# Thirteen buffers for the attention rows, stores issued later, and the turned keys copied by ScalarE

## The chip, the cores and the metric

The kernel is one program on one core of a Trainium2 chip. The metric is device time in microseconds (us), from a launch with all inputs in device memory to the last output row. Before the change the median of three runs is 881.03 us (880.51 to 882.46).

## What the kernel computes

Three stages in a row, on 3072 tokens of 384 features (4 batches x 768 positions, 8 heads of 48):

```
# 1. gated linear attention, per batch and head
f = 1 / (1 + exp(-f_logit))
state = f[t][:, None] * state + k[t] outer v[t]        # 48 x 48, t = 0..767
y[t] = q[t] @ state
# 2. mixture of 8 experts with a fixed capacity of 384 tokens
x = y as rows [3072, 384];  logits = x @ w_gate
assign tokens greedily, best logits first, until each expert has 384
out[tokens of e] = relu(x[tokens of e] @ w1[e]) @ w2[e]
# 3. a dense layer pair on all tokens
h = x @ w_in;  g = h * tanh(log(1 + exp(h)));  g @ w_out
```

Inputs are float32 but for `w_in` and `w_out`, which arrive as 8-byte floats and are split into a high and a low part on the chip.

## The kernel before

The attention stage takes the first 164 us. It walks through 24 units; unit u is a pair (chunk c of 128 positions, batch b), c = u // 4 and b = u % 4. A unit has these steps, each a few instructions: the gates (`gate1`, `gate2`: exponential, minimum, logarithm of the gate inputs, split into `sphi` and `splo`), their running sum on TensorE (`cum`), two exponentials of it (`ep`, `kp`), the products with q and k on GpSimd, the turning of both (`trans`: eight 128x128 transposes into two PSUM tiles, then copies to `qT` and `kT`), the scores `sc` = kT x qT, their mask `scm`, the output `y`, the state's update, and `rows`, which turns the output back into token rows, writes the logits to `L` and the rows through `xs` to `x_rows` in device memory.

The steps of several units are interleaved. In the loop over u a string of letters, `ORD = "tcHOkEPyrCseimaQSnNoxDpMdb"`, is the order in which work is given to the engines in one unit: a small letter with a step beside it emits TensorE work, and the capital and other letters flush work that was deferred (a copy out of PSUM, a mask). So unit u emits the transposes of u+1, the running sum of u+2, the rows of u-1, the output of u and the scores of u+1. Every engine runs its own instructions strictly in this order.

The parts that the change touches:

- `trans` (line 413): the copy to `qT` is deferred under letter H and done by ScalarE (line 423); the copy to `kT`, under letter O, is done by VectorE (line 424). In VectorE's list it stands behind the splitting of the 8-byte weights (lines 84 to 86) and behind one step of `fill` (lines 153 to 176, constants for the routing), which end the unit before, and ahead of the reduction to `L`, the gates' minimum, the state's addition (line 468) and `sphi` (line 361).
- `rows` (line 475): `xs` has two buffers, and the store of 128 rows of 1536 bytes is issued at once, in unit u for the rows of u-1.
- The loop head (lines 546 to 551): the loads of `f` for unit u+6, of q, k and v for u+4 and a piece of the 8-byte weights, all on SyncE's queue, as are the stores and the small transfer `decs` (line 379), which brings the last row of `ep` to four partitions. At b = 2 `dec` (line 384) reads four such rows of a chunk.

Transfers issued by SyncE take eight completion semaphores in turn: each issue first waits until the transfer eight places before it has landed.

After the attention a branch on `flag` picks a slow path that these inputs don't take. The routing then sorts out the tokens of the first expert, gathers their rows from `x_rows` (line 907) and the expert stage runs to the end.

Of the kernel before, what the change touches and what calls it, by code (L numbers as in the profile page):

```python
# [7 lines left out]
F32 = mybir.dt.float32  # L8
# [5 lines left out]
AF = mybir.ActivationFunctionType  # L14
# [216 lines left out]
def tile_gated_attention(ctx, tc, q, k, v, f_logit, w_gate, x_d, L, flag, ident, fill, one, w64, choices):  # L231
# [5 lines left out]
    nc = tc.nc  # L237
    B, H, S, D = q.shape
    C = 128
    NC = S // C  # L240
    DP = 64
    NP = H // 2
# [4 lines left out]
    work = ctx.enter_context(tc.tile_pool(name="a_work", bufs=2))  # L247
# [5 lines left out]
    NU = len(units)  # L253
# [22 lines left out]
    def load_f(u):  # L276
        if u >= NU:
            return
        f = work.tile([128, H, D], F32, name="f", bufs=4)
        nc.sync.dma_start(f, src(f_logit, u))  # L280
        F[u] = f

    def load(u):
        if u >= NU:
            return
        kk = work.tile([128, H, D], F32, name="kk", bufs=3)
        qq = work.tile([128, H, D], F32, name="qq", bufs=3)
        nc.sync.dma_start(qq, src(q, u))
        nc.sync.dma_start(kk, src(k, u))
        LD[u] = (kk, qq)  # L290

    def load_v(u):
        if u < NU:
            nc.sync.dma_start(vv[u % NV], src(v, u))
# [46 lines left out]
    def misc(shape):  # L341
        return psum.tile(shape, F32, name="misc", bufs=2)
# [24 lines left out]
    def cum(u):  # L367
        c, b = units[u]
        kk, qq = LD[u]
        hi, lo = SP[u]  # L370
        pc = psum.tile([128, H, D], F32, name="cum")
        pcf = pc.rearrange("p h d -> p (h d)")
        nc.tensor.matmul(pcf, trir, hi, start=True, stop=False)
        nc.tensor.matmul(pcf, trir, lo, start=False, stop=True)
        def exps():
            ep = epad[u % 2]
            nc.scalar.activation(ep[:, :, :D], pc, AF.Exp, scale=-1.0)
            nc.scalar.activation(kpad[u % 3][:, :, :D], pc, AF.Exp)
            (nc.scalar if u < 4 else nc.sync).dma_start(decr[c % 2][b:b + 1], ep[127:128])
            defer("P", lambda: (nc.vector if u < 2 else nc.gpsimd).tensor_mul(qpad[u % 2][:, :, :D], qq, ep[:, :, :D]))  # L380
            defer("Q", lambda: (nc.vector if u < 1 else nc.gpsimd).tensor_mul(kpad[u % 3][:, :, :D], kk, kpad[u % 3][:, :, :D]))
        defer("E", exps)

    def dec(c):
        V = nc.vector
        r = slice(c % 2 * 32, c % 2 * 32 + B)
        V.tensor_scalar(fjunk[r], decr[c % 2][:, :, :D], 1e-34, None, op0=OP.is_ge, op1=OP.min,
                        accum_out=flg[r, c:c + 1])
        V.tensor_scalar(flg[r, c:c + 1], flg[r, c:c + 1], -1.0, 1.0, op0=OP.mult, op1=OP.add)
        if c == NC - 1:  # L390
            return
        p = misc([128, NP, B])
        for j in range(NP):
            nc.tensor.transpose(p[:, j, :], decr[c % 2][:, 2 * j:2 * j + 2, :].rearrange("b h d -> b (h d)"), ident[r, r])
        d = work.tile([128, NP, B], F32, name="dec")
        V.tensor_copy(d, p)
        DEC[c] = d
# [10 lines left out]
    def set_flag2(m):  # L408
        p = misc([1, 1])
        nc.tensor.matmul(p, m, ident_ones, start=True, stop=True)  # L410
        nc.vector.tensor_scalar(flag, p, 1.0, None, op0=OP.min)

    def trans(u):
        pq = psum.tile([128, NP, 128], F32, name="tr", bufs=2)
        for j in range(NP):
            nc.tensor.transpose(pq[:, j, :], qpad[u % 2][:, 2 * j:2 * j + 2, :].rearrange("p h d -> p (h d)"), ident)
        pk = psum.tile([128, NP, 128], F32, name="tr", bufs=2)
        for j in range(NP):
            nc.tensor.transpose(pk[:, j, :], kpad[u % 3][:, 2 * j:2 * j + 2, :].rearrange("p h d -> p (h d)"), ident)
        qT = work.tile([128, NP, 128], F32, name="qT")  # L420
        kT = work.tile([128, NP, 128], F32, name="kT")
        QT[u], KT[u] = qT, kT
        defer("H", lambda: nc.scalar.activation(qT, pq, AF.Copy))
        defer("O", lambda: nc.vector.tensor_copy(kT, pk))

    def scores(u):

# [12 lines left out]
    def yout(u):  # L440
        c, b = units[u]
        p = py


        for j in range(NP):
            for s in range(2):
                nc.tensor.matmul(p[s * DP:s * DP + D, j], vv[u % NV][:, 2 * j + s, :], SC[u][:, 2 * j + s, :],
                                 start=j == 0, stop=not c and j == NP - 1)
        for j in range(NP if c else 0):
            for s in range(2):  # L450
                r = slice(s * DP, s * DP + D)
                nc.tensor.matmul(p[r, j], St[b][r, j, :], QT[u][r, j, :], start=False, stop=j == NP - 1)
        def copy():
            xT = work.tile([128, NP, 128], F32, name="xT", bufs=1)
            nc.scalar.activation(xT, p, AF.Copy)
            XT[u] = xT
        defer("x", copy)

    def state(u):
        c, b = units[u]  # L460
        if c == NC - 1:
            return
        p = misc([128, NP, DP])
        for h in range(H):
            s, j = h % 2, h // 2
            nc.tensor.matmul(p[s * DP:(s + 1) * DP, j, :D], kpad[u % 3][:, h, :],
                             vv[u % NV][:, h, :], start=True, stop=True)
        defer("a", lambda: nc.vector.tensor_add(St[b], St[b], p[:, :, :D]))

    def decay(u):  # L470
        c, b = units[u]
        nc.gpsimd.tensor_mul(St[b], St[b], DEC[c][:, :, b:b + 1].to_broadcast([128, NP, D]))

    def rows(u):

        c, b = units[u]
        p = misc([128, NP, PW])
        for j in range(NP):
            nc.tensor.matmul(p[:, j, :], XT[u][:, j, :], pick[:, j, :], start=True, stop=True)
        def store():  # L480
            xs = work.tile([128, NP, 2 * D], F32, name="xs")
            nc.scalar.activation(xs, p[:, :, :2 * D], AF.Copy)
            r0 = b * S + c * C
            nc.sync.dma_start(x_d[r0:r0 + C, :], xs.rearrange("p j d -> p (j d)"))
        defer("r", store)
        defer("C", lambda: nc.vector.tensor_reduce(L[:, b * NC + c, :], p[:, :, 2 * D:].rearrange("p j e -> p e j"),
                                                   axis=AX.X, op=OP.add))
# [4 lines left out]
    def defer(letter, fn):  # L492
        if now[0] or letter not in ORD:
            fn()
        else:
            pend.setdefault(letter, []).append(fn)

    def flush(letter=None):
        for l in list(pend) if letter is None else [letter]:
            while pend.get(l):  # L500
                pend[l].pop(0)()
# [39 lines left out]
    for u in range(NU):  # L541
        c, b = units[u]
        if u == 3:
            filling = fill(jp)
        if u >= 3 and b != 2:
            next(filling, None)
        load_f(u + 6)
        load(u + 4)
        load_v(u + 4)
        if u >= 3:  # L550
            w64.step("load")
        now[0] = False
        for o in ORD:
            flush(o)
            if o in 'mbp' and u < 3:
                continue
            if o == 'm':
                w64.step("magnitude")
            if o == 't' and u + 1 < NU:
                trans(u + 1)  # L560
            if o == 'c' and u + 2 < NU:
                cum(u + 2)
            if o == 'b':
                w64.step("bits")
                if u == last:
                    w64.step("parts")
            if o == 'y':
                yout(u)
                if u == last:
                    set_flag2(far)  # L570
            if o == 's':
                state(u)
            if o == 'D' and b == 2:
                dec(c)
            if o == 'e':
                gates(min(u + 5 - (u < 2), NU), 0)
            if o == 'n':
                gates(0, min(u + 4, NU))
            if o == 'k' and u:
                rows(u - 1)  # L580
            if o == 'p':
                w64.step("parts")
            if o == 'S' and u < last:
                scores(u + 1)
            if o == 'd':
                decays(u)
        if u == NU - 2:
            far = set_flag()
    flush()
    now[0] = True  # L590
    for _ in filling:
        pass
    rows(NU - 1)
    for _ in choices.steps(work.tile([128, H, D], F32, name="qq", bufs=3).rearrange("p h d -> p (h d)")):
        pass
    while not w64.done():
# [740 lines left out]
```

## Time and profile before

| | us |
|---|---|
| median of three runs | 881.03 (880.51 to 882.46) |
| the profiled execution | 884.77 |
| its span, first to last instruction | 882.8 |
| TensorE busy | 821.2 (93%) |
| VectorE busy | 680.2 (77%) |
| ScalarE busy | 541.8 (61%) |
| GpSimd busy | 401.8 (46%) |

Times in the traces are those of the one profiled execution. "Busy" is an average over stages; in the slices of the page the DMA engines are full (digit 9) only in the first six of 40, which is the attention stage. A wait that a view names is put down to the semaphore that came last.

### The profile page before, as it was taken

How to read it: one execution, taken by the hardware profiler on the slowest of the kernel's cores; microseconds unless marked ns; L12 is line 12 of the kernel's file. 1: busy time of each engine (PE TensorE's matmuls, PEld its weight loads, DVE VectorE, ACT ScalarE, POOL GpSimd, SP SyncE). 2: the span in 40 equal slices, each digit the busy share in tenths (PEclk: the TensorE clock that was granted, in tenths of full speed). 3: DMA queues.
4: the chain of work that ended last, by engine and by line, in shares of the span. 5: the costliest groups of instructions: out<-in, count | busy, mean ns of one | idle time of the engine just before them, and what ended most of it. 6: DMA issues, size and time to landing. Idle time of an engine off the chain costs nothing.

```text
span 882.8 us, 16971 instructions
## 1 busy us (share of the span) xinstructions
PE 821.2 (93%) x6162; PEld 766.9 (87%) x6162; DVE 680.2 (77%) x1734; ACT 541.8 (61%) x1283; POOL 401.8 (46%) x395
## 2 busy tenths in 40 slices
PE   7989999548999999999999999999999999999996
PEld 6878888446888889999989998899889899999995
DVE  5668898778799869876987798779877885765564
ACT  5656666215378538754774587467637764884684
POOL 4657788134237423641464155415532643545143
PEclk9999999768999999999999999999999999999999
DMA  9999995253330003001300210030004105100000
GB/s 166 200 225 218 215 220 135 84 157 120 130 104 27 1 28 144 27 10 29 133 28 19 103 60 19 28 143 19 9 29 144 27 1 171 27 1 25 4 1 27
DMA packets 127862, 71.97 MB, mean 82 GB/s; under 512 B 102944, under 2 KB 120352, under 8 KB 127776
## 3 DMA queue, kind: packets, MB, share of 16 engines
q1 hardware_dynamic: 124576, 61.41, 26.3%
q0 software_dynamic: 3072, 9.44, 3.4%
q8 instruction: 50, 0.82, 0.4%
q14 instruction: 36, 0.29, 0.1%
q10 hardware_dynamic: 128, 0.01, 0.0%
HBM read 61.35 MB, written 9.44 MB: 80 GB/s over the span
## 4 chain that ended last, share of the span: by engine, by line
PE 51%; issue 9%; POOL 9%; DVE 5%; DMA 3%; ACT 2%; POOLq 0%; SPq 0%; DVEq 0%; ACTq 0%
PE h L947 17%; PE h L945 9%; PE acc L947 8%; POOL gl L1014 6%; PE acc L1069 4%; PE acc L945 4%; PE acc L1064 4%; PE acc L1065 4%; DMA xg<-x_rows,idx 2%; POOL xg L907 1%; POOL w1l L915 1%; DVE cmp L696 1%; PE misc L773 1%; DMA w1r<-in_moe_w_dram 1%; ACT gh L1005 1%
## 5 line engine op out<-in xcount | busy, mean ns | idle before, releaser
L1014 POOL TENSOR_TENSOR gl<-g,gh 128x384 fp32r<-128x384 f32 x127 | 162.8, 1282 | 288.9 <-ACT gh L1005 284.3
L945 PE MATMUL h<-yh,winh 128*128 128x384 f32 x384 | 132.5, 345 | 0.3 <-DVE g L995 0.2
L1064 PE MATMUL acc<-wouth,gh 128*128 128x384 f32 x384 | 130.1, 339 | 1.1 <-ACT gh L1005 0.5
L947 PE MATMUL h<-yh,winl 128*128 128x384 f32 x384 | 129.4, 337 | 0.0
L1065 PE MATMUL acc<-woutl,gh 128*128 128x384 f32 x384 | 129.4, 337 | 0.0
L947 PE MATMUL h<-yl,winh 128*128 128x384 f32 x384 | 129.3, 337 | 0.0
L1034 DVE SCALAR_TENSOR_TENSOR e<-e,r 128x384 f32<-128x384 f32 (+2 forms) x154 | 78.2, 522 | 34.7 <-ACT r L1029 34.2
L963 ACT ACTIVATE h1h<-h 128x384 fp32r<-128x384 f32 x64 | 31.4, 491 | 112.8 <-PE h L947 112.7
L915 POOL TENSOR_TENSOR w1l<-w1r,w1h 128x384 fp32r<-128x384 f32 x64 | 67.4, 1054 | 72.4 <-ACT w1h L914 72.4
L1069 PE MATMUL acc<-wouth,gl 128*128 128x384 f32 x384 | 89.5, 341 | 1.8 <-POOL gl L1014 1.7
L1022 ACT ACTIVATE e<-e 128x384 f32<-128x384 f32 (+2 forms) x154 | 69.5, 468 | 29.9 <-DVE e L1043 27.8
L1005 ACT ACTIVATE gh<-g 128x384 fp32r<-128x384 f32 (+2 forms) x154 | 69.0, 464 | 28.4 <-DVE g L995 27.8
L1047 DVE SCALAR_TENSOR_TENSOR e<-e,r 128x384 f32<-128x384 f32 (+2 forms) x154 | 82.2, 548 | 0.2
L1040 ACT ACTIVATE e<-h 128x384 f32<-128x384 f32 (+2 forms) x154 | 62.7, 424 | 23.7 <-PE h L947 23.7
L1064 PEld LDWEIGHTS acc<-wouth,gh 128*128 128x128 f32 x384 | 72.0, 188 | 4.5 <-ACT gh L1005 4.5
L995 DVE SCALAR_TENSOR_TENSOR g<-e,h 128x384 f32<-128x384 f32 (+2 forms) x154 | 71.8, 480 | 4.1
L1043 DVE TENSOR_SCALAR e<-e 128x384 f32<-128x384 f32 (+2 forms) x154 | 58.5, 391 | 21.3 <-ACT e L1040 21.1
L945 PEld LDWEIGHTS h<-yh,winh 128*128 128x128 f32 x384 | 72.5, 189 | 1.7 <-issue 0.7
L947 PEld LDWEIGHTS h<-yl,winh 128*128 128x128 f32 x384 | 72.2, 188 | 0.8
L1069 PEld LDWEIGHTS acc<-wouth,gl 128*128 128x128 f32 x384 | 67.3, 188 | 5.9 <-POOL gl L1014 5.3
L1065 PEld LDWEIGHTS acc<-woutl,gh 128*128 128x128 f32 x384 | 72.1, 188 | 0.0
L947 PEld LDWEIGHTS h<-yh,winl 128*128 128x128 f32 x384 | 72.0, 188 | 0.0
(239 smaller groups left out, 2052.2 us busy)
## 6 DMA issues: line engine op xcount, KB each, us to landing
w1r<-in_moe_w_dram SPq DMA_DIRECT2D x8, 1536.0 KB, 6.4
w2r<-in_moe_w_dram SPq DMA_DIRECT2D x8, 1536.0 KB, 9.6
f<-in_f_logit_dram SPq DMA_DIRECT2D x24, 192.0 KB, 3.8
qq<-in_q_dram SPq DMA_DIRECT2D x24, 192.0 KB, 4.2
kk<-in_k_dram SPq DMA_DIRECT2D x24, 192.0 KB, 4.5
vp<-in_v_dram SPq DMA_DIRECT2D x24, 192.0 KB, 4.4
x_rows<-xs SPq DMA_DIRECT2D x24, 192.0 KB, 3.2
cv_raw<-in_moe_w_in_dram SPq DMA_DIRECT2D x9, 384.0 KB, 4.3
```

Of the source, the lines that this page charges most:

```text
L915: nc.gpsimd.tensor_sub(al, s, ah.bitcast(F32))
L945: nc.tensor.matmul(p, wh, xh, start=start, stop=False)
L947: nc.tensor.matmul(p, w, x, start=False, stop=stop and w is (wh if late_x else wl))
L995: nc.vector.scalar_tensor_tensor(g[:, c], s2[:, c], 0.5, p[:, c], op0=OP.add, op1=OP.mult)
L1005: nc.scalar.activation(gh[:, c], g[:, c], AF.Copy)
L1014: nc.gpsimd.tensor_sub(gl, g, gh.bitcast(F32))
L1022: nc.scalar.activation(s[:, c], s[:, c], AF.Square, bias=1.0)
L1034: nc.vector.scalar_tensor_tensor(s[:, c], s[:, c], 1.0, r[:, c], op0=OP.add, op1=OP.mult)
L1047: nc.vector.scalar_tensor_tensor(s[:, c], s[:, c], 2.0, r[:, c], op0=OP.subtract, op1=OP.mult)
L1064: nc.tensor.matmul(A[k, 1][t], gh[:, s], wouth[:, f, :], start=f == 0, stop=False)
L1065: nc.tensor.matmul(A[k, 1][t], gh[:, s], woutl[:, f, :], start=False, stop=False)
L1069: nc.tensor.matmul(A[k, 1][t], gl[:, s], wouth[:, f, :], start=False, stop=f == GB - 1)
```

## The change

The rows of up to thirteen units stay in SBUF: `xs` gets 13 buffers, and `rows` no longer issues the store but puts it on a list. From the thirteenth unit (u = 12) on, the loop head takes one store off the list per unit and issues it, behind that unit's loads; from u = 19 on it takes up to four. What is left is issued after the last rows. Apart from that the copy to `kT` goes from VectorE to ScalarE, at the same letter.

```diff
         defer("H", lambda: nc.scalar.activation(qT, pq, AF.Copy))
-        defer("O", lambda: nc.vector.tensor_copy(kT, pk))
+        defer("O", lambda: nc.scalar.activation(kT, pk, AF.Copy))
...
+    NX = 13
+    stores = []
+
+    def put_rows(n):
+        for _ in range(min(n, len(stores))):
+            nc.sync.dma_start(*stores.pop(0))
+
     def rows(u):
...
-            xs = work.tile([128, NP, 2 * D], F32, name="xs")
+            xs = work.tile([128, NP, 2 * D], F32, name="xs", bufs=NX)
             nc.scalar.activation(xs, p[:, :, :2 * D], AF.Copy)
             r0 = b * S + c * C
-            nc.sync.dma_start(x_d[r0:r0 + C, :], xs.rearrange("p j d -> p (j d)"))
+            stores.append((x_d[r0:r0 + C, :], xs.rearrange("p j d -> p (j d)")))
...
         if u >= 3:
             w64.step("load")
+        if u >= NX - 1:
+            put_rows(1 if u < NU - 5 else 4)
         now[0] = False
...
     rows(NU - 1)
+    put_rows(NU)
```

On SyncE's queue, around units 2 and 3, the instructions stood like this before (L280, L288, L289 and L294 load f, q, k and v, L60 the 8-byte weights, L379 is `decs`, L484 the store of rows):

```order
L484 DMA x_rows<-xs 128x384
L280 DMA f<-in_f_logit_dram 128x8x48
L288 DMA qq<-in_q_dram 128x8x48
L289 DMA kk<-in_k_dram 128x8x48
L294 DMA vp_103<-in_v_dram 128x8x48
L60 DMA cv_raw<-in_moe_w_in_dram 128x3x256
L379 DMA decs<-ep_113 1x16x32
L484 DMA x_rows<-xs 128x384
L280 DMA f<-in_f_logit_dram 128x8x48
```

Now the first store on this queue is that of unit 12; the end of the loop, from the loads of unit 19 on, reads so (L480 is the store):

```order
L288 DMA qq<-in_q_dram 128x8x48
L289 DMA kk<-in_k_dram 128x8x48
L294 DMA vp_104<-in_v_dram 128x8x48
L60 DMA cv_raw<-in_moe_w_in_dram 128x3x256
L480 DMA x_rows<-xs 128x384 x4
L379 DMA decs<-ep_113 1x16x32
L60 DMA cv_raw<-in_moe_w_out_dram 128x768
L480 DMA x_rows<-xs 128x384 x4
L379 DMA decs<-ep_112 1x16x32
L480 DMA x_rows<-xs 128x384 x4
L379 DMA decs<-ep_113 1x16x32
L480 DMA x_rows<-xs 128x384 x4
```

Up to unit 11 a unit's round on the queue has six transfers in place of seven; the stores of 17 of the 24 units now stand behind the last load of q, k and v.

On VectorE, around the thirteenth unit, where `fill` has its longest step (L173), the copy L424 is gone from between that step and the reduction to `L` (L486, now L494):

```order
 L86 SCALAR_TENSOR_TENSOR cv_x<-cv_x,cv_s 128x384
 L173 CAST slots<-row 128x512
-L424 COPY kT<-tr 128x512
-L486 TENSOR_REDUCE L<-misc 128x8
+L494 TENSOR_REDUCE L<-misc 128x8
 L351 TENSOR_SCALAR f<-f 128x384
 L468 TENSOR_TENSOR S_114<-S_114,misc 128x192
```

Nothing else moves in that list. On ScalarE the copy now stands right behind its twin L423 and ahead of the two exponentials of the running sum:

```order
 L423 ACTIVATE qT<-tr 128x512
+L424 ACTIVATE kT<-tr 128x512
 L377 ACTIVATE ep_113<-cum 128x8x48
 L378 ACTIVATE kp_108<-cum 128x8x48
 L379 DMA decs<-ep_113 1x16x32
-L482 ACTIVATE xs<-misc 128x384
+L490 ACTIVATE xs<-misc 128x384
 L348 ACTIVATE f,esum<-f 128x384
```

So the exponentials, and behind them the copy to `xs` and the gates, start one copy later in ScalarE's list.

## Rows read from the trace of the kernel before

**Rows 1.** The page: span, and DMA busy tenths in 40 slices

```profile
span 882.8 us, 16971 instructions
DMA  9999995253330003001300210030004105100000
```

**Rows 2.** Stretches: length, busy PE, PEld, DVE, ACT, POOL, PE clock, DMA share, GB/s

```profile
74.50:92.80 18.30, 18.30 (x253) 16.30 (x254) 14.94 (x33) 13.09 (x31) 14.48 (x16) 1.00 0.96 218
92.80:112.30 19.50, 18.30 (x251) 16.26 (x250) 18.35 (x35) 12.97 (x31) 15.69 (x18) 1.00 0.97 219
112.30:132.20 19.90, 18.10 (x247) 16.03 (x247) 18.57 (x32) 13.11 (x31) 16.05 (x18) 1.00 0.97 216
180.00:200.00 20.00, 11.11 (x104) 9.57 (x102) 14.22 (x58) 3.19 (x7) 6.23 (x7) 0.68 0.57 181
```

**Rows 3.** Waits of PE, 15 to 150 us: total, times, longest

```profile
PE sc L432 <- DVE L L486: 4.1, 6, 1.2
PE misc L394 <- issue: 2.6, 1, 2.6
PE sc L432 <- ACT wouth L107: 0.5, 1, 0.5
```

**Rows 4.** Timeline of the thirteenth unit, all engines: start, duration, instruction, wait

```profile
94.34 1.23 DVE L173 CAST slots<-row 128x512 bf16<-128x512 f32 x1
94.77 0.67 PE L466 MATMUL misc<-vp,kp 128*64 128x48 f32 x16
95.49 0.68 DVE L424 COPY kT<-tr 128x512 f32<-128x512 f32 x1
96.31 1.16 PE L432 MATMUL sc<-qT,kT 48*128 48x128 f32 x16 [0.87 <-DVE L L486]
96.72 0.35 DVE L361 CAST sphi<-f 128x384 fp32r<-128x384 f32 x1
97.21 1.00 POOL L364 TENSOR_TENSOR splo<-f,sphi 128x384 fp32r<-128x384 f32 x1 [1.93 <-DVE sphi L361]
98.51 0.34 PE L374 MATMUL cum<-splo,trir 128*128 128x384 f32 x1
```

**Rows 5.** Timeline of units 5 and 6, PE and SyncE's queue

```profile
43.20 1.08 PE L447 MATMUL y<-scm,vp 128*48 128x128 f32 x16
49.16 1.08 PE L447 MATMUL y<-scm,vp 128*48 128x128 f32 x16
51.78 1.16 PE L432 MATMUL sc<-qT,kT 48*128 48x128 f32 x16
51.85 0.51 SPq L379 DMA_DIRECT2D decs<-ep  x1
55.59 0.38 PE L394 MATMUL misc<-ident,decs 4*128 4x4 f32 x4 [2.65 <-issue]
```

**Rows 6.** Two stretches that follow waits of PE, columns as in Rows 2

```profile
55.60:60.00 4.40, 4.40 (x28) 4.20 (x30) 4.20 (x15) 1.74 (x4) 2.01 (x4) 0.61 1.08 230
69.60:74.00 4.40, 4.39 (x30) 4.18 (x31) 3.41 (x8) 0.82 (x2) 2.77 (x4) 0.61 0.86 219
```

**Rows 7.** The line of the stores, 20 to 52 us: count, ns, starts

```profile
L484 SPq DMA_DIRECT2D x_rows<-xs x4: 518/526/1999, 27.4 to 47.3; - x4
```

**Rows 8.** Timeline of the fourteenth unit: ScalarE, GpSimd and the next transposes

```profile
98.10 0.60 ACT L423 ACTIVATE qT<-tr 128x512 f32<-128x512 f32 x1 [2.20 <-PE tr L416]
98.89 0.49 ACT L377 ACTIVATE ep<-cum 128x384 f32<-128x384 f32 x1 [0.19 <-PE cum L374]
101.47 1.32 POOL L381 TENSOR_TENSOR kp<-kk,kp 128x384 f32<-128x384 f32 x1
103.77 0.66 PE L416 MATMUL tr<-ident,qp 128*128 128x128 f32 x4
```

**Rows 9.** Timeline of the stage's end: the last `xs`, then the first gather

```profile
163.79 0.49 ACT L482 ACTIVATE xs<-misc 128x384 f32<-128x384 f32 x1 [0.82 <-PE misc L479]
190.06 1.18 POOL L907 DMA_INDIRECT xg<-x_rows,idx  x1 [10.67 <-DVE th L868]
```

## The prediction

> **What bounds the kernel now.** I read the page first: the span is 882.8 us, and the DMA engines are full in the first six of 40 slices only, the attention stage [rows 1]. Everything that the change touches lies in that stage, which ends with the last copy to `xs` at 163.79 + 0.49 = 164.3 us [rows 9]. Next I cut the stage into stretches of three units each. From 74.5 to 92.8 us TensorE is busy 18.30 of 18.30 us, at full clock, with the DMA engines at 0.96; in the two stretches after it TensorE idles 1.20 and 1.80 us while VectorE is busy 18.35 of 19.50 and 18.57 of 19.90 [rows 2]. So two things run close together here: TensorE's own work and the transfers. Which one ends last must be read from TensorE's waits. An undisturbed unit is the distance between two outputs, 49.16 - 43.20 = 5.96 us, without a gap [rows 5].
>
> TensorE's waits from 15 to 150 us come third. Two kinds carry nearly everything: the scores wait for VectorE or, by the label, for ScalarE, 4.1 + 0.5 = 4.6 us in seven places, and the transposes of `decs` wait once, 2.6 us [rows 3]. The label of the scores' wait names the instruction that came last by the profile, and I read it further in the timeline: in the thirteenth unit the state's matmuls end at 94.77 + 0.67 = 95.44; the copy to `kT`, an operand of the scores, stands behind the 1.23 us step of `fill`, ends at 95.49 + 0.68 = 96.17, and the scores start at 96.31 [rows 4]. They wait for `kT`. The wait for `decs` is another story: the transfer is issued at 51.85, TensorE is through with its scores at 51.78 + 1.16 = 52.94 and starts the transposes at 55.59, 3.74 us after the issue [rows 5].
>
> Behind two of these waits there is a second loss: from 55.6 to 60.0 and from 69.6 to 74.0 us TensorE is busy throughout, but at a mean granted clock of 0.61 [rows 6]; each follows a wait, the one for `decs` and the longest of the scores (1.2 us). The two levels are 1.2 and 2.4 GHz, so 0.61 is mostly the lower one. Each stretch loses 4.4 x (1 - 0.61) = 1.7 us, if its work scales with the clock.
>
> **The change part by part.**
>
> The copy to `kT`. VectorE loses 24 copies of 0.68 us, ScalarE gains 24 of the same shape as its copy to `qT`, 0.60 us [rows 4, 8]. On VectorE the copy stood ahead of the scores; now it is done right behind `qT`, at 98.70 to 99.30 in the unit shown, over 3 us ahead of those scores. All 4.6 us of waits go [rows 3], and I expect the second stretch of low clock to go with the wait ahead of it: 1.7 us [rows 6]. What is late next is the low half of the running sum, which takes `splo` from GpSimd, which takes `sphi` from VectorE. In the thirteenth unit `sphi` ends at 97.07, 0.90 after the copy ended; without it VectorE is through with the `fill` step at 95.57 and `sphi` ends about 96.47, so `splo`, 0.14 us later and 1.00 long, ends at 97.61. TensorE takes its scores at 95.44 and, 98.51 - 96.31 = 2.20 us later, asks for `splo` at 97.64 [rows 4]. That just fits. Where VectorE's list is longer relative to TensorE's it won't, and I allow 0.6 us in all for such places; the ends are 0 and 3.0 us, the idle time of TensorE in the two stretches where VectorE is fullest [rows 2].
>
> On ScalarE the copy delays `ep` from 98.89 to 99.30, 0.41 us, since 0.19 us of waiting is used up [rows 8]. Busy time per unit was 13.09 / 3 = 4.36 us [rows 2], so 4.96 of 5.96 then. Queued behind are `kp`, `xs`, the gates and `xT`, and `ep` releases GpSimd's two products. In the unit shown the second of them ends at 101.47 + 1.32 = 102.79, while the next transposes start at 103.77 [rows 8]: 0.98 us of cover against 0.41 of delay. I cost it at nothing; if the cover is gone, the price is up to 0.41 us a unit.
>
> The stores. What they cost before is their share of a full DMA. A store is 128 x 1536 bytes = 197 KB. No row isolates it, so I bound it: at the mixed rate of the full stretches, 218 GB/s at share 0.96, it is 0.87 us; at the rate that large pieces reach later, 181 GB/s at a share of 0.57, that is 318 GB/s at full, 0.62 us [rows 2]. Its rows are large pieces, so I take 0.62. Issuing one also holds SyncE's queue 0.53 us [rows 7]. With the engines full and eight transfers under way at most, whatever is taken out ahead of a transfer brings it forward. Four stores stood ahead of the `decs` that TensorE waited for [rows 7]: at 0.62 us they are 2.5 us, at 0.87 it is 3.5. The transfer would be issued at 49.35 or earlier and land, with the same 3.74 us, at 53.09, against TensorE's 52.94 [rows 5]. I count 2.2 of the 2.65 us as gone, with 0 and 2.65 as ends, and the low clock after it gone with it, 1.7 us [rows 6].
>
> The Trainium skill, "DMA: Bandwidth & Descriptors", section Specifications, puts the ceiling of the fabric at 435 GB/s. By that a store would be an estimated 0.45 us, four 1.8, and the wait would keep some 0.8 us, so that the sum below came out 0.4 lower; the fastest stretch cited here stands at 318 GB/s, and the trace decides for the larger price.
>
> From unit 12 on one store a unit comes back, into a queue which by then has caught up, and the four per unit from 19 on stand behind the last loads. Three small losses are possible: `decs` of the last chunks stands behind four issues of 0.53 us, and the routing's first instructions wait for every landed store. I allow 0.3 us. The first gather starts at 190.06, 25.8 us after the last `xs` [rows 9]; 16 late stores at 0.62 to 0.87 us are 10 to 14 us of DMA time, spread over the last five units, so the gather doesn't see them. Everything after the stage moves as a block.
>
> Sum: 4.6 + 1.7 + 2.2 + 1.7 - 0.6 - 0.3 = 9.3 us. Against the profiled execution this is 882.8 - 9.3 = 873.5 us of span and 884.77 - 9.3 = 875.5 us in all; that execution is 3.7 us above the median of the runs, so 881.03 - 9.3 = 871.7 us is what I predict.
>
> **The rivals.**
>
> (A) The wait for `decs` stays or moves. The DMA engines remain near full, and with a faster TensorE the transfers have less time; from unit 12 on the stores are back. Then 2.2 + 1.7 us are not gained, and the change brings 5.4: 875.6 us. For it: DMA shares of 0.96 and 0.97 up to 132 us [rows 2]. Against it: removing one of seven transfers cuts a unit's demand below its 5.96 us.
>
> (B) VectorE stays the bound where GpSimd is busiest. VectorE's busy time per unit rises from 14.94 / 3 = 4.98 us to 18.35 / 3 = 6.1 and 18.57 / 3 = 6.2 as GpSimd's goes from 4.83 to 5.23 and 5.35 [rows 2]; the one long `fill` step is only 1.23 of it [rows 4]. Closer packing could stretch it again until the freed 0.68 us is eaten: the 3.0 us of idle time there stays, and the change brings 9.3 - 2.4 = 6.9: 874.1 us. Against it: 6.2 - 0.68 = 5.5 is under 5.96. The Trainium skill, "SBUF — State Buffer", section Terms, has VectorE and GpSimd arbitrate for one shared pair of ports, the loser blocked for a full instruction. By that rule the packing does stretch VectorE, and the time is the 874.1 us of this case; the rise in the rows agrees with it, as far as they go.
>
> (C) The stores pile up at the end. Sixteen are issued in the last five units and the branch's far side waits for all. If four are still queued behind the last one, 4 x 0.62 to 0.87 adds 2.5 to 3.5 us to the routing's start: 9.3 - 3 = 6.3, 874.7 us.
>
> (D) Slower. ScalarE paces the units: what `ep` loses to the copy holds GpSimd's products, these the next transposes, these the next copies, and the delay is handed on from unit to unit. It decides from the point where `ep` is late by more than the 0.98 us of cover [rows 8]; the copy alone gives 0.41, so the gates and `xT` behind it would have to slip too. Then the units, now (18.3 + 19.5 + 19.9) / 9 = 6.41 us on average [rows 2], last 0.60 us more instead of getting shorter: 20 units with a state part lose 12.0 us, the relief at `decs` still brings 3.9, and the time is 881.03 + 8.1 = 889.1 us. Against it: a ScalarE that even with the copy idles 1.0 us of each 5.96.
>
> **How the numbers follow.** The forecast with both mechanisms, a gain of 8 to 11 us, gets 0.60; A 0.15, B 0.10, C 0.06, D 0.04; 0.05 is left for something that I don't see and that leaves no change. The range runs from a gain of 11.7 us (all bounds at their best, 4.6 + 1.7 + 2.65 + 1.7 = 10.65, and 1.1 for unseen relief of the early transfers) to one of 4.2, somewhat under A: 869.3 to 876.8 us. About 0.2% of the time, 1.8 us, is what can be told from no change; faster by more gets 0.91, within it 0.05, slower 0.04.
>
> **What would show it.** Right: outputs 5.96 us apart from unit 4 to unit 20, but for some 0.3 us at each `dec`; no wait of the scores for VectorE; the wait for `decs` under 0.6 us; a granted clock of 1.00 from 20 us to the stage's end; the last `xs` at about 155 us; every later stage of its old length. Wrong: a new wait of the running sum for `splo` over 1 us in total (B), of the transposes for GpSimd (D), of `decs` in unit 10, 14 or 18 (A), or a routing that starts over 3.5 us after the last `xs` (C).

## The result

The changed kernel took 872.66 us (median of 4 runs, 871.43 to 874.92) against 880.85 us of the kernel before (4 runs): a ratio of 0.9893, 95% interval 0.9869 to 0.9917, a gain of 8.2 us. Measured again beside the later experiments it took 874.20 us against 881.46, a ratio of 0.9926 (0.9896 to 0.9955). The forecast was 871.7.

The page after: 13.1 us less span, and the DMA engines are still full in the first six slices [rows 1].

```profile
span 869.7 us, 16917 instructions
DMA  9999996362510021003100400031004105000000
```

The end of the attention stage, the last `xs` and the first gather [rows 9]:

```profile
154.85 0.49 ACT L490 ACTIVATE xs<-misc 128x384 f32<-128x384 f32 x1 [0.81 <-PE misc L487]
181.17 1.19 POOL L918 DMA_INDIRECT xg<-x_rows,idx  x1 [10.68 <-DVE th L879]
```

The stage ends at 155.34 instead of 164.28 us, 8.94 earlier, and the gather starts 8.89 earlier: the stores that are still out when the stage ends cost the routing nothing. Nothing shows that the rest of the 13.1 us belongs to the change. From the first expert's first gather to the second's, in code that did not change, the profile of before took 76.74 us and this one 72.90; over the thirteen profiles of this study that stretch took 72.2 to 76.7, in no order that follows the edits. The medians, 8.2 us apart, agree with the stage alone.

TensorE's waits from 15 to 150 us, after (total, times, longest) [rows 3], and the stretches of rows 2 between the same outputs:

```profile
PE cum L374 <- POOL splo L364: 1.2, 3, 0.6
```

```profile
74.75:93.17 18.42, 18.42 (x251) 16.26 (x250) 16.22 (x33) 14.01 (x34) 15.06 (x17) 1.00 0.95 204
93.17:111.74 18.57, 18.48 (x251) 16.27 (x250) 17.26 (x32) 14.13 (x34) 15.72 (x18) 1.00 0.93 197
111.74:129.96 18.22, 18.22 (x251) 16.26 (x250) 15.80 (x33) 13.72 (x34) 16.37 (x18) 1.00 1.00 227
...
20.00:155.00 135.00, 132.91 (x1773) 117.37 (x1770) 106.03 (x224) 97.76 (x230) 100.85 (x113) 1.00 0.91 204
```

The waits of the scores and of `decs` are gone, TensorE is busy 55.12 of the 55.21 us of the three stretches (columns: length, busy PE, PEld, DVE, ACT, POOL, PE clock, DMA share, GB/s), and its granted clock is at 1.00 from 20 us to the end of the stage. The thirteenth unit [rows 4], the copy now on ScalarE:

```profile
88.61 1.22 DVE L173 CAST slots<-row 128x512 bf16<-128x512 f32 x1
89.03 0.67 PE L466 MATMUL misc<-vp,kp 128*64 128x48 f32 x16
89.63 1.16 PE L432 MATMUL sc<-qT,kT 48*128 48x128 f32 x16
...
90.38 0.34 DVE L361 CAST sphi<-f 128x384 fp32r<-128x384 f32 x1
90.87 1.01 POOL L364 TENSOR_TENSOR splo<-f,sphi 128x384 fp32r<-128x384 f32 x1 [1.32 <-DVE sphi L361]
91.91 0.59 ACT L424 ACTIVATE kT<-tr 128x512 f32<-128x512 f32 x1
91.93 0.19 PEld L374 LDWEIGHTS cum<-splo,trir 128*128 128x128 f32 x1 [0.20 <-POOL splo L364]
```

The scores start with no gap behind the state's matmuls, while `fill`'s long step is still running on VectorE. `splo` is now what comes last, and by little: TensorE's weight load waits 0.20 us for it. In two other units it waits longer:

```profile
67.55 0.19 PEld L374 LDWEIGHTS cum<-splo,trir 128*128 128x128 f32 x1 [0.56 <-POOL splo L364]
110.50 0.19 PEld L374 LDWEIGHTS cum<-splo,trir 128*128 128x128 f32 x1 [0.35 <-POOL splo L364]
```

These waits hardly show in TensorE's busy time, in which matmuls overlap, but the three units last 6.53, 6.16 and 6.32 us from output to output in place of 5.96, 1.1 us more in all. Waits for `splo` aren't new, either. The view from which rows 3 are taken has this line too:

```profile
PE cum L374 <- POOL splo L364: 1.6, 3, 0.6
```

Those three waits of before, and two of the three after, lie in the stage's first units, up to 27 us. Units 5 and 6 [rows 5], and the stretch behind the transposes of `decs` [rows 6]:

```profile
48.65 0.50 SPq L379 DMA_DIRECT2D decs<-ep  x1
50.01 1.08 PE L447 MATMUL y<-scm,vp 128*48 128x128 f32 x16
52.63 1.16 PE L432 MATMUL sc<-qT,kT 48*128 48x128 f32 x16
53.73 0.41 PE L394 MATMUL misc<-ident,decs 4*128 4x4 f32 x4
```

```profile
53.70:58.10 4.40, 4.40 (x54) 4.07 (x54) 4.24 (x12) 3.35 (x9) 4.40 (x6) 1.00 1.06 241
```

`decs` is sent 1.36 us ahead of the unit's output, where before it was sent 2.69 behind it, and L394 doesn't wait. The same 4.4 us now hold 54 matmuls where they held 28.

### The profile page after: what moved, and what is told of

The parts are those of the page before. It is cut to its first block, busy times and chain, and to the rows that moved or that the text cites. A ratio compares the mean times of both kernels' runs of the same rounds, so it can differ in the third digit from the quotient of the medians.

```text
span 869.7 us, 16917 instructions
## 1 busy us (share of the span) xinstructions
PE 817.1 (94%) x6162; PEld 763.7 (88%) x6162; DVE 670.5 (77%) x1710; ACT 551.1 (63%) x1307; POOL 403.7 (46%) x395
## 4 chain that ended last, share of the span: by engine, by line
PE 54%; POOL 8%; issue 8%; DVE 5%; DMA 3%; ACT 2%; POOLq 0%; SPq 0%; DVEq 0%; ACTq 0%
PE h L958 18%; PE h L956 10%; PE acc L958 7%; POOL gl L1025 5%; PE acc L1080 5%; PE acc L1075 4%; PE acc L1076 4%; PE acc L956 4%; DMA xg<-x_rows,idx 2%; POOL xg L918 2%; DVE cmp L707 1%; POOL w1l L926 1%; PE misc L784 1%; DMA w2r<-in_moe_w_dram 1%; ACT e L1051 1%
```

## What the experiments showed

`decs` collects the last row of `ep` from four units; the row of the last of the four (u = 7, 11, 15, 19, with u counted from 0) is the one that L394 can be late for. The table puts all kernels side by side, each from its own profile: from the first `y` to the last `xs`, how long after the end of `ep` (L377) that unit's row was sent (L379), and how long TensorE stood for it. The ratio is to the kernel before on the same chip.

| kernel | ratio (95%) | first y to last xs | row sent after ep, u = 7, 11, 15, 19 | waits at L394 |
|---|---|---|---|---|
| before | 1 | 148.95 | 7.91, 2.71, 3.19, 2.78 | 2.65 |
| changed | 0.9893 (0.9869 to 0.9917) | 139.14 | 4.67, 2.69, 4.54, 5.57 | none |
| changed, again | 0.9926 (0.9896 to 0.9955) | 139.90 | 6.31, 4.16, 5.09, 5.97 | 0.20 |
| keys alone | 0.9959 (0.9940 to 0.9977) | 143.80 | 6.35, 5.56, 6.58, 4.38 | 0.76, 2.47 |
| stores alone | 0.9979 (0.9964 to 0.9993) | 148.81 | 7.20, 1.66, 3.52, 4.69 | 1.52 |
| VectorE's copy placed earlier | 0.9969 (0.9953 to 0.9985) | 143.24 | 7.25, 5.93, 4.97, 5.60 | 1.23, 0.58 |
| changed, 7 buffers | 0.9954 (0.9932 to 0.9976) | 145.93 | 6.55, 6.47, 5.86, 8.03 | 0.32, 2.18, 1.57 |
| keys, row by ScalarE | 0.9911 (0.9882 to 0.9941) | 140.40 | 0.03 each | none |
| row by ScalarE alone | 0.9953 (0.9930 to 0.9975) | 143.51 | 0.03 each | none |
| changed, row by ScalarE | 0.9909 (0.9877 to 0.9942) | 140.14 | 0.03 each | none |
| changed, copied twice | 0.9921 (0.9901 to 0.9941) | 142.08 | 4.17, 2.81, 3.99, 6.94 | 1.49 |
| the same, row by ScalarE | 0.9928 (0.9902 to 0.9953) | 141.20 | 0.03 each | none |
| changed, first three keys by VectorE | 0.9909 (0.9884 to 0.9934) | 140.16 | 6.04, 3.75, 4.65, 6.33 | 0.30 |

Waits under 0.1 us are left out. Every such row that was sent 6.35 us or more after its `ep` made TensorE wait, and none that was sent within 5.9 us did. In the cases with a wait TensorE was ready for the row 9.0 to 10.2 us after that `ep`, and the row took 3.5 to 5.8 us from issue to landing: it is late when standing in line and landing together take longer than TensorE leaves them.

Lengths and rows are those of one execution for each kernel; the two of the changed kernel differ by 0.76 us in length and by 1.64 us in when the row of u = 7 was sent. The ratios rest on 4 to 12 runs of each kernel.

### Keys alone

```diff
-        defer("O", lambda: nc.vector.tensor_copy(kT, pk))
+        defer("O", lambda: nc.scalar.activation(kT, pk, AF.Copy))
```

> Only the copy to kT goes to ScalarE; the stores stay as before. Theory (two separate causes): the scores' seven waits of 4.6 us go, and the low clock behind the longest with them (1.7 us); the wait for decs in unit 6 stays at 2 to 3.5 us, since it comes ahead of most of the others. Last xs ends at 157.5 to 159.5 us instead of 164.3 (155.3 with both parts), the time is some 875.5 us. Rival (the transfers set the pace): TensorE gets ahead and waits for decs in units 10, 14 or 18 too, over 1 us each; last xs after 160.5 us, time above 877.

The stage ended at 159.92 us, between the two theories, and the time, 878.62 us, was in the rival's range. TensorE's waits, its clock behind the longer of the two, and SyncE's line ahead of it:

```profile
PE misc L394 <- issue: 3.2, 2, 2.5
...
```

```profile
93.27 0.49 ACT L377 ACTIVATE ep<-cum 128x384 f32<-128x384 f32 x1
93.80 0.60 SPq L379 DMA_DIRECT2D decs<-ep  x1
...
99.64 0.60 SPq L60 DMA_DIRECT2D cv_raw<-in_moe_w_in_dram  x1
100.34 0.51 SPq L379 DMA_DIRECT2D decs<-ep  x1
106.25 0.44 PE L394 MATMUL misc<-ident,decs 4*128 4x4 f32 x4 [2.47 <-issue]
```

```profile
106.30:110.70 4.40, 4.40 (x28) 4.28 (x30) 3.16 (x9) 2.29 (x5) 2.01 (x3) 0.61 0.87 220
```

The scores wait for nothing any more, but the wait for `decs` moved from unit 6, where 0.76 us of it is left, to unit 14: the row of u = 15 was ready at 93.76 and stood in SyncE's line for 6.58 us (the row sent at 93.80 is that of u = 14). This is rival A's mechanism. Two things made the wait. SyncE issued six other transfers between the two rows, and the seven issues by themselves took 5.95 of the 6.54 us; the eight semaphores held none of them up, since no issue of the stage began less than 1.89 us after the transfer eight places before it had landed. And this row was slow to land, 5.82 us where the median is 3.7. At the median TensorE would have waited some 0.4 us, an estimate (2.47 - 2.1).

### Stores alone

The changed kernel with the line of the keys as before (`nc.vector.tensor_copy(kT, pk)`).

> Only the stores are held back; the copy to kT stays on VectorE. Theory: the wait for decs in unit 6 (2.65 us) and the low clock behind it (1.7 us) go; the scores' waits for kT stay at 4 us or more in total, among them the one of 1.2 us with low clock behind it. Last xs ends at 159.5 to 161 us, the time is some 877 us. Rival (the transfers set the pace, the copy hardly counts): the scores' waits shrink as well, last xs under 158 us, time 874 or less.

Almost nothing came of it in the profile: the stage ended 0.45 us earlier, in the range of neither theory, and 0.31 of that is an earlier first `y` (15.02 us, before 15.33). By the times it gained somewhat more, 1.45 us between the medians, 0.6 to 3.2 by the interval.

```profile
PE sc L432 <- DVE L L494: 4.2, 6, 1.2
...
PE misc L394 <- DMA decs<-ep: 1.5, 1, 1.5
```

```profile
49.80 0.50 SPq L379 DMA_DIRECT2D decs<-ep  x1
51.45 1.16 PE L432 MATMUL sc<-qT,kT 48*128 48x128 f32 x16
54.14 0.56 PE L394 MATMUL misc<-ident,decs 4*128 4x4 f32 x4 [1.52 <-DMA decs<-ep]
```

```profile
54.10:58.50 4.40, 4.36 (x22) 4.38 (x22) 4.15 (x14) 1.47 (x3) 1.56 (x4) 0.50 1.03 212
58.10:60.10 2.00, 2.00 (x16) 1.80 (x17) 1.69 (x4) 1.21 (x5) 1.69 (x2) 0.50 0.96 193
```

With four stores out of its way the row went 51.85 - 49.80 = 2.05 us earlier, or 1.73 us against the output of its own unit (49.16 before, 48.84 here). Of these, 0.56 went into a slower landing (4.21 us, before 3.65). So the wait shrank by 1.13 us, to 1.52, and did not go. The low clock behind it stayed (0.50, against 0.61 in rows 6) and lasted longer: here it was still 0.50 from 58.1 to 60.1 us, while before it was back at 0.94 from 59.6 to 61.6. So 0.48 of the 1.13 us reached the next output (y(6) to y(7) took 9.99 us, before 10.47), and y(7) to y(8) lost more than that again (6.84 us, before 6.05). The output of unit 8 came when it had come before; first this kernel, then the kernel before:

```profile
65.67 1.08 PE L447 MATMUL y<-scm,vp 128*48 128x128 f32 x16
```

```profile
65.68 1.08 PE L447 MATMUL y<-scm,vp 128*48 128x128 f32 x16
```

### VectorE's copy, placed earlier

VectorE keeps the copy, but the weights' splitting and the step of `fill` are given out one letter later than the copy (and `cv_raw` has four buffers in place of three).

```diff
-    ORD = "tcHOkEPyrCseimaQSnNoxDpMdb"
+    ORD = "tcHObkEPyrCseimaQSnNoxDpMd"
...
-        if u >= 3 and b != 2:
-            next(filling, None)
...
+            if o == 'b' and b != 2:
+                next(filling, None)
```

> Before, with the copy to kT still on VectorE but ahead of the weight splitting and of fill in its list (the letter b, with fill, moves from the end of a unit to behind letter O; the split of a piece of weights runs one unit later, with a fourth buffer for the raw weights). Theory (the copy's place in the list was the fault, not VectorE's load): the scores' waits for kT go as in the kernel with the keys alone, last xs at 157.5 to 160 us. Rival (VectorE is full): the waits come back at other instructions, the running sum waits over 2 us in total for splo, last xs after 161 us.

TensorE's waits from 15 to 150 us:

```profile
PE cum L374 <- POOL splo L364: 1.3, 5, 0.3
PE misc L394 <- issue: 1.2, 1, 1.2
PE misc L394 <- DMA f<-in_f_logit_dram: 0.6, 1, 0.6
```

No wait of the scores is left, the stage ended at 158.73 us, and the waits for `decs` are 1.23 and 0.58 us. So the scores waited because of the copy's place in VectorE's list. As to the stage's length it did as much as taking the copy off VectorE (143.24 and 143.80 us).

### Seven buffers

```diff
-    NX = 13
+    NX = 7
```

> The changed kernel with 7 buffers in place of 13: one store a unit already from unit 6 on. Theory (what counts is the relief ahead of decs in unit 6; later the queue keeps up): no wait for decs over 0.5 us anywhere, last xs within 0.7 us of the 155.3 of the changed kernel, time about 872.5 us. Rival (the transfers are the bound until the stores stop): waits for decs of 1 us or more in units 10, 14 or 18, last xs at 157 us or later, time 874.5 or more.

With a store a unit back from u = 6 on, the waits for `decs` are back in units 10 and 18, and the stage ended at 161.35 us, past the rival's bound. The one of 2.18 us is again that of a row slow to land (sent after 6.47 us, landed 5.64 us later), the one of 1.57 us that of a row sent late (8.03 and 3.47 us). So on top of the keys it does matter how long the stores stay out.

### Keys on ScalarE, and the row sent by ScalarE

The kernel of the keys alone, stores at once and two buffers, with one more edit:

```diff
-            (nc.scalar if u < 4 else nc.sync).dma_start(decr[c % 2][b:b + 1], ep[127:128])
+            nc.scalar.dma_start(decr[c % 2][b:b + 1], ep[127:128])
```

> The turned keys are copied by ScalarE and every unit stores its rows at once, as in the run with the keys alone (last xs done 159.92, TensorE's row misc L394 3.2 us in 2 waits, one of them 2.47 in the fourteenth unit); but the decs row is always sent by ScalarE's queue, not by SyncE's from the fifth unit on. Theory 1 (the row stands in line behind loads and stores of SyncE's queue, so the wait is one of place): misc L394 falls under 0.6 us, the low clock behind it goes, last xs done at 155 to 157, time 872 to 876. Rival (the 16 DMA engines are full, whoever issues the row finds no gap): misc L394 stays over 1.5 us in one or two units between the sixth and the eighteenth, last xs done after 158.5, time 877 to 880, as with the keys alone.

The stage ended at 155.77 us, at 873.05 us in all, without any of the thirteen buffers. TensorE's waits and the row of u = 15:

```profile
PE cum L374 <- POOL splo L364: 1.0, 4, 0.3
PE cum L374 <- DMA f<-in_f_logit_dram: 0.5, 1, 0.5
```

```profile
92.03 0.49 ACT L377 ACTIVATE ep<-cum 128x384 f32<-128x384 f32 x1
92.56 0.50 ACTq L379 DMA_DIRECT2D decs<-ep  x1
...
102.80 0.41 PE L394 MATMUL misc<-ident,decs 4*128 4x4 f32 x4
```

The transfers of L379 from issue to landing, here and with the keys alone:

```profile
DMA to landing us min/median/max: 1.7/3.6/4.6
```

```profile
DMA to landing us min/median/max: 1.6/3.7/5.8
```

The medians differ by 0.1 us: who issues the row changes little in how long it takes once it is issued, and much in when it is sent. The row's place in SyncE's line is what this edit cures. A slow landing had a part in the waits all the same, since the 5.8 us above is that of the row behind the 2.47 us. Here the row of u = 15 had landed 4.0 us after its `ep` and L394 came 6.3 us behind, so even such a landing would not have been late. The Trainium skill, "DMA: Bandwidth & Descriptors", section Rules for kernel authors, says of spreading transfers over the issuing engines that it doesn't help for bandwidth and only saves issue time. For bandwidth no run here speaks against it (DMA share from 20 to 155 us 0.88 with the keys alone, 0.90 here); what one small row saved here was the 6.55 us that it had stood in line (6.58 to 0.03), and with them went two waits.

### The row by ScalarE alone, and with everything

The same edit on the kernel before, and on the changed kernel.

> The kernel before (VectorE copies the turned keys, every unit stores its rows at once) with one edit: the decs row is always sent by ScalarE's queue. In the kernel before SyncE sent the row of the eighth unit 7.91 us after its ep was done and TensorE stood 2.65 us for it; with the keys on ScalarE and this edit it is sent 0.03 us after ep in every unit. Theory (two separate costs of about the same size; the row's place in SyncE's line is one of them): no misc L394 wait over 0.5 us, the wait of 2.65 and the low clock behind it (about 1.7) go, the waits of sc for VectorE (4.1 us) and the low clock at 69.6:74 stay, last xs done at 159.4 to 160.6 against 164.28, time 876 to 878.5. Rival (VectorE's copy holds the pace, as when the stores alone were held back, and the wait only changes its name): last xs done after 163, time 880 to 882.

> The changed kernel with the decs row always sent by ScalarE's queue, so the keys on ScalarE, the stores held back and the row out of SyncE's line. Theory (held stores and a row of its own queue cure the same wait, and one cure is enough): last xs done at 155.0 to 156.0 as with either alone (155.34 and 155.77), time 872 to 874, the same as the changed kernel's. Rival (each still leaves something to the other: with the stores out of the way k and v come sooner too): last xs done before 154.5, time 871 or less.

Alone it ended the stage at 158.95 us, a little earlier than the theory had it, and shortened first y to last xs by 5.44 us, about as much as the keys alone (5.15; the ratios, 0.9953 and 0.9959, don't tell them apart). The scores' waits stayed, but the low clock that the theory expected did not: there was none behind the longest of them, which stands here, nor elsewhere from 20 to 155 us (1.00):

```profile
PE sc L432 <- DVE L L486: 5.0, 7, 1.3
```

```profile
66.05 1.16 PE L432 MATMUL sc<-qT,kT 48*128 48x128 f32 x16 [1.25 <-DVE L L486]
```

```profile
66.05:70.45 4.40, 4.40 (x52) 3.99 (x54) 3.88 (x8) 2.17 (x5) 3.51 (x5) 1.00 0.95 227
```

On the changed kernel it brought nothing that can be told (872.55 us, stage end 155.32): held stores and a queue of its own cure the same wait.

### The keys copied twice by ScalarE

```diff
-        defer("O", lambda: nc.scalar.activation(kT, pk, AF.Copy))
+        defer("O", lambda: (nc.scalar.activation(kT, pk, AF.Copy), nc.scalar.activation(kT, pk, AF.Copy)))
```

> The changed kernel, with ScalarE's copy of the turned keys made twice in each unit (the second writes the same values again): 0.60 us more of ScalarE a unit, in 24 units 14.4 us. Theory (ScalarE has room: 15.85 us busy of 20 in the stretch 80:100 of the changed kernel, 4.8 of the 6.1 us a unit takes, so 5.4 with the second copy): last xs done at 154.5 to 156.5, no wait of TensorE's scores for ScalarE over 1 us in all, time 871 to 874. Rival D (ScalarE paces, so that what is added to it shows): units of 6.2 us or more throughout, last xs done after 158, waits of sc for ACT of 2 us or more, time 875 to 885.

> The changed kernel with ScalarE's copy of the turned keys made twice a unit, as in the earlier run of that edit (last xs done 158.73, first y 16.65, a misc L394 wait of 1.49 us in the twentieth unit, whose row was sent 6.94 us after its ep), and the decs row always sent by ScalarE's queue. Theory (ScalarE's second copy cost time only because a row that was on the edge came late to SyncE's line): no misc L394 wait over 0.5 us, the unit of 7.82 us is gone, last xs done 1.5 to 2.5 us earlier, at 156 to 157.2, time 872.5 to 874. Rival D (ScalarE paces: 0.60 us more in each unit shows however the row goes): last xs done after 158, first y to last y over 136.5 us, time 875 or more.

14.4 us more work on ScalarE made first y to last xs 2.2 to 2.9 us longer, 1.49 of it one wait: the row of u = 19 was sent 6.94 us after its `ep`. The stage's end, 158.73 us, is past rival D's mark of 158, but no scores waited for ScalarE. With the row on ScalarE's queue that wait is gone (stage end 157.40, 0.2 past the theory's range), and 1.06 us remain against the changed kernel with that edit, 0.89 of it from y(0) to y(4) (22.79 against 21.90 us). ScalarE does not pace the units behind these.

### The changed kernel again, and VectorE for the first three keys

```diff
-        defer("O", lambda: nc.scalar.activation(kT, pk, AF.Copy))
+        defer("O", lambda: nc.vector.tensor_copy(kT, pk) if u < 3 else nc.scalar.activation(kT, pk, AF.Copy))
```

> The changed kernel, but VectorE copies the turned keys of the first three units, ScalarE those of the other 21. The first y of the changed kernel came at 16.20, of the kernel before at 15.33. Theory (in the first unit ScalarE copies the keys behind the turned queries, one after the other, and the scores wait for it): first y at 15.0 to 15.6, last xs done 0.6 to 0.9 earlier than in the changed kernel of the same chip, time 871.8 against 872.7. Rival (the early matmuls ran slower in that one run and ScalarE's place has no part in it): first y anywhere from 15.0 to 16.2 in both, time within 0.4 us of the changed kernel's.

> The changed kernel once more, on the chip of the three others, so that their times and traces stand beside its own. Theory (the gain lies in the attention units and repeats): last xs done at 154.5 to 156.3, no wait of scores for VectorE, TensorE's row misc L394 under 0.6 us, time 0.989 to 0.992 of the kernel before. Rival (the one profile showed a lucky run; the held stores don't always keep the decs row on time): a misc L394 wait of 1.5 us or more in one unit, last xs done after 157.5. Of the 3.84 us that the first profile gained between 190 and 267 us both say nothing; if it comes from the clock of that run and not from the change, it needn't come again.

The first `y` came at 15.46 us in the repetition and at 15.64 with VectorE's early copies, the stages ended at 155.36 and 155.80: the late start of the first profile (16.20) was that run's own and not ScalarE's doing. The repetition bears out the stage's gain (9.05 us from first `y` to last `xs`, after 9.81), and shows how close it runs: the row of u = 7 was sent 6.31 us after its `ep`, and TensorE stood 0.20 us for it. None of the variants is faster than the changed kernel by more than their intervals.

## Why the prediction was right, and where it was wrong

Right by the traces: the total (9.3 us; 9.81 and 9.05 measured in the stage from the first `y` on, 8.2 and 7.3 between the medians of the times); the waits of the scores, read as waits for `kT`, gone; nothing lost at the stage's end (C, where 17 stores, not sixteen, were issued from unit 19 on); none of ScalarE's delay handed on (D).

About `splo` it was half right. "Two kinds carry nearly everything" passed over 1.6 us of waits for `splo` and 0.3 for `sphi` in the same view. So B's mark, a new wait for `splo` of over 1 us in total, could not tell: the total was 1.6 us before and is 1.2 and 1.7 now. By the length of the units `splo` cost 1.1 us behind the first units, against 0.6 allowed; but in the two stretches on which B rests it cost 0.35 us, where B had 3.0.

Wrong in how the total is made up. That it came out is in part luck: what the stores alone did not bring, they brought on top of the keys.

- "Four stores stood ahead ... I count 2.2 of the 2.65 us as gone ... and the low clock after it gone with it." Together with the late losses this made 2.2 + 1.7 - 0.3 = 3.6 us for the stores. Alone they gave 0.14 us in the profile (148.95 to 148.81) and 1.45 us by the times. The step that failed is "land, with the same 3.74 us", and with it the low clock "gone with it": landing took 0.56 us longer, 1.52 us of waiting was left, and the low clock behind it lasted longer than before.
- In the same term, four stores were sized at 2.5 us, and the row was brought forward by 1.73. By the prediction's own numbers 0.15 us of the wait was left (53.09 against 52.94); it gives no reason for entering 2.2 and not 2.5. That the stores cost the row their DMA time is not shown, either: four issues of 0.53 us that SyncE is spared, 2.1 us, fit as well. And "eight transfers under way at most" bounded nothing: in the profile of before no issue of the stage began less than 1.72 us after the transfer eight places before it had landed.
- The low clock at 69.6:74 was charged to the scores' wait ahead of it. With the row sent by ScalarE, that wait (1.25 us) and its six like were still there, 5.0 us in all, and the clock was at 1.00. With the stores alone, and so a wait for `decs` of 1.52 us before it, it was at 0.66 in that stretch. What it hung on is not shown, but not on the scores' wait by itself.
- "Into a queue which by then has caught up." It did not stay so: the row went 2.69 us after `ep` at u = 11, but, with stores back, 4.54 at u = 15 and 5.57 at u = 19 (5.97 in the repetition), some 0.4 us from where waits begin.
- The terms were summed as if each stood alone. Keys alone 5.15 and stores alone 0.14 make 5.3 of 9.8; after the keys, holding the stores was worth 4.66 (143.80 to 139.14). The times show it less sharply: between the medians 4.07 and 1.45 us alone, 8.2 and 7.3 together. With shorter units SyncE's line has less time for its transfers, so the late row comes back as in A (with the keys alone 5.56 and 6.58 us after `ep` at u = 11 and 15, before 2.71 and 3.19), unless the stores stay out of the line long enough. A was given 0.15 and judged by DMA share. The share is as high in the kernel where the wait is gone; the row's place in SyncE's line was what to look at, and L379's start against the end of `ep` would have shown it: 7.91 us in the trace of before.

What isn't settled: why holding the stores moves the row by so different amounts (sent 4.67 and 6.31 us after `ep` at u = 7 in two runs of one program, 7.20 with VectorE's copy), why single rows took 5.6 and 5.8 us to land, and what made the stretch between the first two experts' gathers differ by up to 4.5 us.

## What to carry to other kernels

For a small transfer on which the busiest engine waits, compare its issue with the moment its data is ready before blaming bandwidth: here, once the keys were on ScalarE, one word (the queue that sends the row) did as much as eleven more buffers and the moving of 24 stores. Don't add up waits that share a queue: the wait you cure lets the engine run into the next, and half of a cure can be worth little. And when a copy makes an engine late, its place in the list may matter more than its length.

## What the runs showed of the hardware

A wait of TensorE costs more than its length when the granted clock falls behind it, and its length alone does not say whether it will. Mean clock in the 4.4 us from the wait's end (first three rows: seven buffers; last row: copied twice):

```profile
53.30:57.70 4.40, 4.36 (x52) 4.09 (x54) 4.19 (x12) 3.36 (x9) 3.88 (x6) 1.00 1.05 195
80.30:84.70 4.40, 4.40 (x28) 4.20 (x30) 3.02 (x9) 2.26 (x5) 2.01 (x4) 0.61 0.89 207
133.40:137.80 4.40, 4.38 (x54) 4.10 (x54) 3.70 (x11) 3.38 (x9) 2.48 (x4) 1.00 0.89 203
```

```profile
130.60:135.00 4.40, 4.40 (x54) 4.07 (x54) 3.22 (x11) 3.38 (x9) 1.93 (x4) 1.00 1.00 228
```

Behind waits for `decs` of 2.65, 2.47, 2.18 and 1.52 us the clock was at 0.61, 0.61, 0.61 and 0.50 (the last is the lower level, 1.2 GHz, throughout); behind others of 1.57, 1.49, 1.23, 0.76 and 0.32 it stayed at 1.00, and TensorE got 52 to 54 matmuls into the 4.4 us instead of 22 to 28. Two waits that differ by 0.05 us, 1.52 and 1.57, fell on either side. So did two waits of the scores: 1.25 us with the row sent by ScalarE (1.00 behind it, shown above) and 1.24 us in the kernel before, behind which rows 6 have 0.61:

```profile
69.61 1.67 PE L432 MATMUL sc<-qT,kT 48*128 48x128 f32 x16 [1.24 <-DVE L L486]
```
